# Second attention stage cut into token halves, packed queries loaded two batches at a time

## The chip, the cores and the metric

The kernel runs on one core of one Trainium2 chip. The metric is the device time of one launch in microseconds; of several runs the median is given. Beside it there is one profiled execution, with a time of its own.

## What is computed

A small packed query set p attends to the keys and values, its result serves as keys and values for the full queries q, and two gated layers follow on all tokens.

```python
# q, k, v: (8 batches, 8 heads, 576 tokens, 64); p: (8, 8, 32, 64); float32
def sm_attn(qq, kk, vv):
    s = scale * np.matmul(qq, kk.transpose(0, 1, 3, 2))
    s = s - np.max(s, axis=-1, keepdims=True)
    a = np.exp(s)
    a = a / (np.sum(a, axis=-1, keepdims=True) + 1e-09)
    return np.matmul(a, vv)
p_packed = sm_attn(p, k, v)              # first attention stage
out = sm_attn(q, p_packed, p_packed)     # second attention stage
x = out.transpose(0, 2, 1, 3).reshape(4608, 512)
h = x @ moe_w_in;  x = (h / (1 + np.exp(-h))) @ moe_w_out
h = x @ moe2_w_in; x = (h * np.cos(h)) @ moe2_w_out
# w_in: (512, 2048), w_out: (2048, 512)
```

## The kernel before

Heads are handled in two groups of four (`g` = 0, 1) of each batch `b`. `place_p(b)` loads the packed queries of one batch into `pin` tiles, eight DMAs of 16 KB, and VectorE transposes them into `pbd`. `stage1(b, g)` is the first attention stage: it turns the keys, forms scores against `pbd`, and leaves the packed result in `ppf`. `stage2(b, g)` is the second: it turns q, forms scores of 128 packed rows by 576 tokens in two PSUM banks of 288 tokens, transposes them into 32x32 blocks (`ba` in the first two batches), takes the maximum over 32 (`mxb`), subtracts it, exponentiates on ScalarE, sums (`rsb`), divides, transposes back (`bat`), and splits the result into a rounded tile and its remainder (the two layers of an `a` tile).

The output product of the second stage is folded into the first layer: `products` multiplies `ppf` with w_in, so that `first(s)`, one step of the first layer, is `hb<-a,w` followed by the gate (`gf`, `g`) and `acc<-g,w`. A step takes one block of 288 tokens and one slice of 128 of the 2048 columns. The first pair of batches runs its slices in four parts of four, each over four token blocks: tokens 0 to 287 and 288 to 575 of batch 0, and the same of batch 1. The weights come as words of 64 bits and are decoded on the chip: each slice is loaded (`wd`, `wde`) and takes two ScalarE and three or four VectorE instructions before PE can use it. The second layer (`second`) follows from about half of the span on.

The first two batches run in the class `Boot`: whole rows of k, v and q come into the `bx` tiles by four DMAs of 288 KB each, and PE turns them. From batch 2 on the class `Steady` loads k and q in pieces (`kin`). While PE would otherwise be idle at the start, `fill` puts in products of the identity matrix (`mb<-ident`).

No instruction is issued where the code stands: all are recorded by `Plan`, which gives each a cost (`price`), a due time and its dependences, orders them over all engines by list scheduling, and emits each engine's instructions in that fixed order (`run`). All DMAs stand in the queue of SyncE (SP). Instructions of one engine run strictly in the planned order, so one that waits holds all behind it. A `copy` may go to ScalarE or VectorE; the planner chooses. In the profile nearly all instructions have line 208 (of the recording helper), so tiles are what tells them apart.

Of the kernel before, what the change touches and what calls it, by code (L numbers as in the profile page):

```python
# [12 lines left out]
F32 = mybir.dt.float32  # L13
# [3 lines left out]
AF = mybir.ActivationFunctionType  # L17
ALU = mybir.AluOpType
AX = mybir.AxisListType
# [15 lines left out]
def f32(ap):  # L35

    return ap.bitcast(F32)
# [42 lines left out]
class Plan:  # L80
# [4 lines left out]
    PE, DVE, ACT, POOL, DMA, NONE = "PE", "DVE", "ACT", "POOL", "DMA", "NONE"  # L85
# [72 lines left out]
    def price(self, engine, f, out, ins):  # L158

        n = math.prod(out.shape[1:])  # L160
        m = max([math.prod(x.shape[1:]) for x in ins], default=n)
        sbuf = all(not str(x.space).endswith("PSUM") for x in ins)
        strided = 44 if ins and n >= 96 and ins[0].ap[-1][0] == 2 else 110 if n >= 96 and out.ap[-1][0] > 2 else 0
        if engine == self.PE:
            if f == "transpose":
                return 3 + n / 1.2, 0

            if ins[0].dtype == F32R:
                return n / 2.4 + (18 if n == 512 else 13), 0
            rows, k = out.shape[0], ins[0].shape[0]  # L170
            if rows == 128:
                return n * 3.33 + 10, 0
            if rows == 64:
                return n * 0.82, 0
            return {64: 30 if k == 96 else 37, 288: 65, 512: 117}[n], 0
        if engine == self.DVE:
            if f == "transpose":
                return (67 if sbuf else 160) + n / 0.92, 0
            fast = sbuf and f in ("tensor_copy", "tensor_scalar", "memset") and m == n
            if f == "scalar_tensor_tensor" and sbuf and ins[0].dtype == F32:  # L180
                return 67 + n / 0.53, 0
            return 67 + max(max(m, n) / (1.92 if fast else 0.96), 60 if f == "reciprocal" else 0) + strided, 0
        if engine == self.ACT:
            return (94 if sbuf else 51) + max(m, n) / 1.2 + (190 if f == "accumulate" else 0) + (105 if f == "sin" else 0) + strided, 0
        if engine == self.POOL:
            return 149 + (1.7 if any(0 in [st for st, _ in x.ap] for x in ins) else 2.1) * n, 0
        run = min(map(self.contiguous, (out, *ins)))
        return self.ISSUE, 4 * math.prod(out.shape) / (260 if run >= 128 else 150)
# [217 lines left out]
def attention_mlps_kernel(  # L406
# [13 lines left out]
    B, H, S, D = q.shape  # L420
    NP = p.shape[2]
    NT, DM = out.shape
    DFF = w_in1.shape[1]
    P = 128
    HALF = S // 2

    TA = HALF
    NB = S // 32
# [8 lines left out]
    SCALE = 1.0 / math.sqrt(D)  # L437
# [5 lines left out]
    V, A, T, G, DMA = plan.V, plan.A, plan.T, plan.G, plan.D  # L443
# [4 lines left out]
    def pool(name, side="left", **kw):  # L448
        return tc.tile_pool(name=name, bufs=1, side=side, **kw)

    def ring(ts):

        at = cycle(ts)
        return lambda: next(at)
# [12 lines left out]
    att = top.enter_context(pool("att"))  # L467
# [3 lines left out]
    def tiles(pl, shape, dtype, name, n):  # L471

        ts = [pl.tile(shape, dtype, name=f"{name}{i}") for i in range(n)]
        cells.setdefault(pl, []).extend(t.tensor.name for t in ts)
        return ts


    def place(b, h2):
        return (b + h2) % 2
# [8 lines left out]
    hb = [psum.tile([P, 512], F32, name=f"hb{i}") for i in range(2)]  # L488
# [5 lines left out]
    def group(s):  # L494
        return list(range(4 * s, 4 * s + 4)) + [FC + b * 8 + kc * 4 + s for b in range(2) for kc in range(2)]
# [10 lines left out]
    def change(stack, pools, name, side, new):  # L506


        def f():
            stack.close()  # L510
            pl = ctx.enter_context(pool(name, side, reuse_waits="tile"))
            for x in new:
                x.tile = pl.tile(list(x.ap.shape), x.ap.dtype, name=x.key)

        plan.switch(f, sum([cells[pl] for pl in pools], []), [x.key for x in new])
# [4 lines left out]
    pbds = [const.tile([P, H // 2, 2 * NP], F32, name=f"pbd{i}") for i in range(2)]  # L520
# [7 lines left out]
    def copy(dst, src):  # L528
        with plan.either():
            A.copy(dst, src)  # L530
            V.tensor_copy(dst, src)

    def combine(dst, x, y, op):
        V.tensor_tensor(dst, x, y, op)

    def split(d, x):

        copy(d[:, 0], x)
        combine(d[:, 1], x, f32(d[:, 0]), ALU.subtract)
# [73 lines left out]
        combine(v[1], v[1], v[2], ALU.subtract)  # L613
        put(y[1], 5)

    pins = ring(tiles(att, [P, H // 2, 32], F32, "pin", 2))
    maxes = ring(tiles(att, [P, 2], F32, "mx", 2))
    ms = ring(tiles(att, [P, 1], F32, "m", 2))
    sumss = ring(tiles(att, [P, 1], F32, "sums", 2))
# [1 line left out]
    mx2s = ring(tiles(att, [P, NB], F32, "mxb", 2))  # L621
    rs2s = ring(tiles(att, [P, NB], F32, "rsb", 2))
    ppfs = ring(tiles(att, [P, 2, 2 * NP], F32, "ppf", 4))
    a2s = ring(tiles(a2p, [P, 2, S], F32R, "a2", 4))

    def place_p(b):
        for side in range(2):
            t = pins()
            for h2 in range(2):
                for x in range(2):  # L630
                    r = (h2 ^ side) * 64 + x * 32
                    DMA.dma_start(t[r : r + 32], p[b, h2::2, :, 32 * x : 32 * x + 32].rearrange("j n d -> n j d"))
            for h2 in range(2):
                r, x = slice(64 * (h2 ^ side), 64 * (h2 ^ side) + 64), NP * place(b, h2)
                V.transpose(pbds[b % 2][r, :, x : x + NP], t[r].rearrange("p j d -> p (j d)"))

    def cut(t, shape):
        t = t[:, : math.prod(shape[1:])]
# [5 lines left out]
    class Steady:  # L644

        @staticmethod
        def spot(h2, hf):
            return 64 * (h2 ^ hf), HALF * hf
# [93 lines left out]
    ppf = {}  # L742
    a2 = {}

    def scores(b, keys, queries, bank, spot):

        sts = [bank()[:, :HALF] for _ in range(2)]
        with plan.together():
            for hf, st in enumerate(sts):
                for j in range(2):  # L750
                    for h2 in range(2):
                        (r, c), x = spot(h2, hf), 32 * place(b, h2)
                        T.matmul(
                            st[64 * j + x : 64 * j + x + 32],
                            keys[r : r + 64, j, x : x + 32],
                            queries[j][r : r + 64, c : c + HALF],
                            start=True,
                            stop=True,
                        )
        return sts  # L760
# [50 lines left out]
    def stage2(b, g, bank, mem):  # L811

        qt = mem.turned(q, b, g, bank)
        s = mem.get("s", [P, NB, 32], g)
        sf = s.rearrange("p n r -> p (n r)")
        for hf, st in enumerate(scores(b, ppf[b, g], qt, bank, mem.spot)):
            V.transpose(sf[:, hf * HALF : (hf + 1) * HALF], st)
        mx = mx2s()
        V.tensor_reduce(mx, s, axis=AX.X, op=ALU.max)
        combine(s, s, mx.unsqueeze(2).to_broadcast([P, NB, 32]), ALU.subtract)  # L820
        A.activation(sf, sf, AF.Exp, scale=SCALE)
        rs = rs2s()
        V.tensor_reduce(rs, s, axis=AX.X, op=ALU.add)
        V.tensor_scalar(rs, rs, 1e-9, None, op0=ALU.add)
        V.reciprocal(rs, rs)
        combine(s, s, rs.unsqueeze(2).to_broadcast([P, NB, 32]), ALU.mult)
        at = mem.get("at", [P, S], g)
        V.transpose(at, sf)
        d = a2s()
        split(d, at)  # L830
        a2[b, g] = d


    def mslot(b, kc, s):
# [204 lines left out]
    gt, st, m5s = {}, {}, {}  # L1039
# [80 lines left out]
    boot = Boot()  # L1120
# [8 lines left out]
    def w1_units(s):  # L1129
        ws = [boot_w1() for _ in range(KC)]  # L1130
        for hp in range(KC):
            w1_unit(s, hp, ws[hp])
        return ws
# [10 lines left out]
    V.memset(half_pi, math.pi / 2)  # L1144

    def firsts(b, mem, banks):
        place_p(b)
        for g in range(2):
            stage1(b, g, banks[g], mem)

    def seconds(b):
        for g in range(2):
            stage2(b, g, bank, steady)


    place_p(0)
    boot.load("k", k, 0)
    ws = w1_units(0)
    boot.load("v", v, 0)
    boot.load("q", q, 0)  # L1160
    pairs = [ring([acc[g], acc[2 + g]]) for g in range(2)]
    for g in range(2):
        stage1(0, g, pairs[g], boot)
    for g in range(2):
        stage2(0, g, ring([hb[g], pairs[g]()]), boot)
    products(0, (0,), ws)
    wout1_units(0)
    steady = Steady()
    bank = ring([sb, mb])
    boot.load("k", k, 1)  # L1170
    boot.load("v", v, 1)
    boot.load("q", q, 1)
    firsts(1, boot, [bank, bank])
    products(0, (1,), ws)
    for g in range(2):
        stage2(1, g, bank, boot)
    change(boot_stack, [bpool], "w_b", "right", [W[i] for i in group(1) + group(2)])
    for s in range(1, NG):
        ws = w1_units(s)
# [5 lines left out]
    for b in (2, 3):  # L1185
        firsts(b, steady, [bank, bank])


    for pr in range(NPAIR):
# [14 lines left out]
        for o in range(PAIR[pr + 1] - PAIR[pr]):  # L1204
# [7 lines left out]
            x = o - 48  # L1212
# [51 lines left out]
```

## Time and profile before

| what | value |
|---|---|
| median of 3 runs | 1529.22 us (1528.01 to 1533.76) |
| profiled execution, its own time | 1525.84 us |
| its span, first to last instruction | 1524.1 us |
| PE busy in the span | 1501.3 us, 99% |
| VectorE (DVE) busy | 1150.8 us, 76% |
| ScalarE (ACT) busy | 783.4 us, 51% |
| mean granted TensorE clock | 0.997 of full |

The profiled execution lies 3.4 us below the median of the runs; 1.7 us of it lie outside the span. PE is busy nearly throughout, so what counts is where it isn't, or where it does only fill work: that is the first 100 us.

### The profile page before, as it was taken

Reading aid. Unit: us, or ns where it says so; the run is one execution under the profiler, and the core shown is the slowest. Engines: PE = TensorE matmul, PEld = TensorE weight load, DVE = VectorE, ACT = ScalarE, POOL = GpSimd, SP = SyncE. Lnnn points to the kernel's source line nnn. Section 1 sums busy time; section 2 is a strip of 40 time slices with the busy share of each in tenths; the row PEclk is TensorE's granted clock in tenths of the full one; section 3 lists DMA queues with packets and bytes.
Section 4 is the critical chain, followed back from the end, with each engine's and each line's share of the span. In section 5 each row is a group of like instructions: output and inputs, shape, how many; then the busy total and the mean of one; then the engine's idle time right before and its main releaser. Section 6 shows DMA issues by size and latency. Waiting matters only on the chain.

```text
span 1524.1 us, 30972 instructions
## 1 busy us (share of the span) xinstructions
PE 1501.3 (99%) x11352; PEld 1358.0 (89%) x11352; DVE 1150.8 (76%) x2424; ACT 783.4 (51%) x1683; POOL 0.7 (0%) x6
## 2 busy tenths in 40 slices
PE   8999999999999999999999999999999999999999
PEld 6788878999789998999989999999999999999997
DVE  5998757786788778686377777888887877777665
ACT  5886554555465555555354444544444544444443
POOL 0000000000000000000000000000000000000000
PEclk9899999999999999999999999999999999999999
DMA  8886557555585666453785758778675657575561
GB/s 219 246 250 168 155 113 176 173 131 135 142 229 178 157 138 192 165 189 113 237 256 174 230 178 252 238 232 248 215 216 191 219 174 230 175 230 177 187 191 35
DMA packets 312632, 287.82 MB, mean 189 GB/s; under 512 B 174240, under 2 KB 222880, under 8 KB 312480
## 3 DMA queue, kind: packets, MB, share of 16 engines
q1 hardware_dynamic: 312480, 285.84, 63.0%
q8 instruction: 90, 1.47, 0.4%
q14 instruction: 62, 0.51, 0.1%
HBM read 232.52 MB, written 53.22 MB: 187 GB/s over the span
## 4 chain that ended last, share of the span: by engine, by line
PE 89%; DMA 3%; DVE 2%; SPq 2%; ACT 2%; issue 1%; DVEq 0%; ACTq 0%
PE acc L208 49%; PE hb L208 22%; PE sb L208 10%; PE mb L208 8%; SPq L208 2%; DMA bx<-in_q 1%; DMA wd<-in_moe_w_in 1%; DMA ypart<-ysb 0%; DMA bx<-in_k 0%; DMA bx<-in_v 0%; DMA kin<-in_q 0%; DMA vin<-in_v 0%; DVE r L208 0%; DVE big L208 0%; DVE w L208 0%
## 5 line engine op out<-in xcount | busy, mean ns | idle before, releaser
L208 PE MATMUL acc<-g,w 128*128 128x288 f32 x3072 | 472.1, 297 | 1.6 <-ACT ysb L208 1.1
L208 PEld LDWEIGHTS acc<-g,w 128*128 128x128 f32 x3072 | 425.7, 188 | 30.6 <-issue 19.8
L208 PE MATMUL acc<-w,g 128*128 128x512 f32 x1728 | 431.6, 392 | 0.0
L208 PEld LDWEIGHTS acc<-w,g 128*128 128x128 f32 x1728 | 310.9, 189 | 55.7
L208 PE MATMUL hb<-a,w 128*128 128x288 f32 x1536 | 266.1, 300 | 5.6 <-DVE gf L208 3.7
L208 PEld LDWEIGHTS hb<-a,w 128*128 128x128 f32 x1536 | 223.6, 189 | 21.6 <-issue 8.5
L208 DVE TENSOR_TENSOR g<-gf,g 128x288 fp32r<-128x288 f32 x256 | 115.0, 451 | 59.9 <-PE acc L208 38.7
L208 ACT CAST g<-gf 128x288 fp32r<-128x288 f32 x234 | 101.1, 434 | 112.8 <-PE acc L208 78.3
L208 ACT ACTIVATE gf<-hb 128x288 f32<-128x288 f32 x256 | 103.4, 411 | 101.9 <-PE hb L208 84.1
L208 DVE SCALAR_TENSOR_TENSOR gf<-gf,hb 128x288 f32<-128x288 f32 x256 | 111.6, 449 | 47.8 <-ACT gf L208 46.6
L208 ACT ACTIVATE r<-r,half_pi 128x512 f32<-128x512 f32 x144 | 103.7, 721 | 35.2 <-DVE r L208 35.0
L208 ACT CAST g<-r 128x512 fp32r<-128x512 f32 x144 | 89.5, 621 | 59.0 <-DVE r L208 56.8
L208 PEld LDWEIGHTS hb<-w,w 128*128 128x128 f32 x729 | 103.8, 190 | 7.9
L208 PE MATMUL hb<-w,w 128*128 128x256 f32 x729 | 110.0, 282 | 0.0
L208 DVE TENSOR_TENSOR g<-r,g 128x512 fp32r<-128x512 f32 x144 | 98.8, 687 | 11.0 <-ACT g L208 10.6
L208 DVE SCALAR_TENSOR_TENSOR r<-n,r 128x512 f32<-128x512 int32 x144 | 99.0, 688 | 2.2
L208 ACT ACTIVATE n<-hb 128x512 int32<-128x512 f32 x72 | 43.1, 598 | 112.0 <-PE hb L208 108.3
L208 DVE TENSOR_TENSOR hb<-hb,gf 128x256 f32<-128x256 f32 x72 | 31.1, 432 | 70.9 <-PE hb L208 70.7
L208 ACT ACTIVATE n<-mb 128x512 int32<-128x512 f32 x36 | 21.5, 598 | 93.1 <-PE mb L208 93.1
L208 PE MATMUL mb<-w,w 128*128 128x256 f32 x456 | 65.6, 282 | 0.0
L208 PE MATMUL sb<-w,w 128*128 128x256 f32 x444 | 64.1, 282 | 0.0
L208 DVE TENSOR_SCALAR r<-r 128x512 f32<-128x512 f32 x144 | 60.9, 424 | 2.6
(204 smaller groups left out, 1911.3 us busy)
## 6 DMA issues: line engine op xcount, KB each, us to landing
w<-w2s SPq DMA_DIRECT2D x504, 256.0 KB, 3.6
w2s<-wd SPq DMA_DIRECT2D x28, 512.0 KB, 3.6
wd<-in_moe_w_in SPq DMA_DIRECT2D x24, 512.0 KB, 4.7
w<-w1dram SPq DMA_DIRECT2D x48, 256.0 KB, 3.5
wd<-in_moe_w_out SPq DMA_DIRECT2D x20, 512.0 KB, 4.7
ydram<-ysb SPq DMA_DIRECT2D x64, 144.0 KB, 2.8
raw<-ydram SPq DMA_DIRECT2D x72, 128.0 KB, 3.6
w2dram<-wd SPq DMA_DIRECT2D x16, 512.0 KB, 3.3
```

The lines of the kernel that those rows point to most:

```text
L208: run = lambda: emit(*[real(x) for x in args], **{k: real(x) for k, x in kw.items()})
```

## The change

The second attention stage of a group is written as a function `half(x)` of a token range. For batches 0 and 1 it is called for tokens 0 to 287 and for 288 to 575, later for all 576 at once as before. In batch 0 the first halves of both groups are recorded ahead of the second halves. The packed queries come in `load_p`, once for two batches, into tiles of double size: eight DMAs of 32 KB where two times eight of 16 KB were. Those of batches 0 and 1 are issued by ScalarE, the later ones by SP as before. `load_p(0)` stands behind the load of the keys.

```diff
@@ price
         if engine == self.ACT:
+            if f == "dma_start":
+                return self.ISSUE, 0
...
-    pins = ring(tiles(att, [P, H // 2, 32], F32, "pin", 2))
+    pins = ring(tiles(att, [P, H, 32], F32, "pin", 2))
...
+    def load_p(b):
+        for side in range(2):
+            t = pin[side] = pins()
+            for h2 in range(2):
+                r = 64 * (h2 ^ side)
+                for x in range(2):
+                    (DMA if b else A).dma_start(
+                        t[r + 32 * x : r + 32 * x + 32],
+                        p[b : b + 2, h2::2, :, 32 * x : 32 * x + 32].rearrange("b j n d -> n (b j) d"),
+                    )
...
@@ stage2
-        for hf, st in enumerate(scores(b, ppf[b, g], qt, bank, mem.spot)):
-            V.transpose(sf[:, hf * HALF : (hf + 1) * HALF], st)
-        mx = mx2s()
-        V.tensor_reduce(mx, s, axis=AX.X, op=ALU.max)
-        combine(s, s, mx.unsqueeze(2).to_broadcast([P, NB, 32]), ALU.subtract)
-        A.activation(sf, sf, AF.Exp, scale=SCALE)
...
-        split(d, at)
+        def half(x):
+            k = slice(x.start // 32, x.stop // 32)
+            y = s[:, k]
+            yf = y.rearrange("p n r -> p (n r)")
+            for hf, st in enumerate(sts):
+                a, e = max(x.start, hf * HALF), min(x.stop, hf * HALF + HALF)
+                if a < e:
+                    V.transpose(yf[:, a - x.start : e - x.start], st[:, a - hf * HALF : e - hf * HALF])
+            V.tensor_reduce(mx[:, k], y, axis=AX.X, op=ALU.max)
+            combine(y, y, mx[:, k].unsqueeze(2).to_broadcast([P, k.stop - k.start, 32]), ALU.subtract)
+            A.activation(yf, yf, AF.Exp, scale=SCALE)
+            V.tensor_reduce(rs[:, k], y, axis=AX.X, op=ALU.add)
+            V.tensor_scalar(rs[:, k], rs[:, k], 1e-9, None, op0=ALU.add)
+            V.reciprocal(rs[:, k], rs[:, k])
+            combine(y, y, rs[:, k].unsqueeze(2).to_broadcast([P, k.stop - k.start, 32]), ALU.mult)
+            V.transpose(at[:, x], yf)
+            copy(d[:, 0, x], at[:, x])
+            combine(d[:, 1, x], at[:, x], f32(d[:, 0, x]), ALU.subtract)
+
         a2[b, g] = d
+        return [lambda x=x: half(x) for x in ((slice(0, HALF), slice(HALF, S)) if b < 2 else (slice(0, S),))]
...
-    place_p(0)
     boot.load("k", k, 0)
+    load_p(0)
+    place_p(0)
...
-    for g in range(2):
-        stage2(0, g, ring([hb[g], pairs[g]()]), boot)
+    fs = [stage2(0, g, ring([hb[g], pairs[g]()]), boot) for g in range(2)]
+    for f in sum(map(list, zip(*fs)), []):
+        f()
```

How the planner orders it is seen in each engine's instructions. ScalarE's first ones in the kernel before (`bkt` are turned keys, `pin` the packed queries):

```order
L1259 UNCONDITIONAL_BRANCH
L208 ACT_TABLE_LOAD
L208 COPY bkt_159<-acc_88 128x288
L208 COPY bkt_159<-acc_90 128x288
L208 COPY bkt_160<-acc_88 128x288
```

And in the changed one:

```order
L1286 UNCONDITIONAL_BRANCH
L210 DMA pin_119<-in_p 32x8x32 x4
L210 DMA pin_120<-in_p 32x8x32 x4
L210 ACT_TABLE_LOAD
L210 COPY bkt_159<-acc_88 128x288
```

ScalarE now issues eight DMAs before its first table load and first copy. SP's queue at the start in the kernel before (`bx_156` keys, `bx_157` values, `bx_158` queries; `wd`, `wde` undecoded weights of the first layer):

```order
L208 DMA bx_156<-in_k 96x2x384 x3
L208 DMA pin_119<-in_p 32x4x32 x4
L208 DMA pin_120<-in_p 32x4x32 x4
L208 DMA bx_156<-in_k 96x2x384
L208 DMA bx_157<-in_v 96x2x384 x2
L208 DMA wd_108<-in_moe_w_in 128x1024
L208 DMA wd_109<-in_moe_w_in 128x1024
L208 DMA wde_113<-in_moe_w_in 128x1024
L208 DMA bx_158<-in_q 96x2x384
L208 DMA bx_157<-in_v 96x2x384 x2
L208 DMA wde_114<-in_moe_w_in 128x1024
L208 DMA bx_158<-in_q 96x2x384
```

And in the changed one:

```order
L210 DMA bx_156<-in_k 96x2x384 x4
L210 DMA wd_108<-in_moe_w_in 128x1024
L210 DMA wd_109<-in_moe_w_in 128x1024
L210 DMA bx_157<-in_v 96x2x384 x2
L210 DMA wde_113<-in_moe_w_in 128x1024
L210 DMA bx_157<-in_v 96x2x384 x2
L210 DMA wde_114<-in_moe_w_in 128x1024
L210 DMA bx_158<-in_q 96x2x384 x2
L210 DMA bx_156<-in_k 96x2x384
L210 DMA bx_158<-in_q 96x2x384
```

The eight loads of `pin` are gone from between the third and the fourth load of keys (and eight more, of batch 1, from further down), and all four weights of the first slice group now stand ahead of the first queries. VectorE in the second stage of batch 1, up to the last instruction of group 1 (`a_140`), in the kernel before:

```order
L208 TENSOR_REDUCE rsb_132<-ba_164 128x18
L208 TENSOR_TENSOR ba_163<-ba_163,rsb_131 128x576
L208 TENSOR_SCALAR rsb_132<-rsb_132 128x18
L208 SCALAR_TENSOR_TENSOR wde_114<-wde_114 128x512
L208 RECIPROCAL rsb_132<-rsb_132 128x18
L208 STREAM_TRANSPOSE bat_165<-ba_163 128x576
L208 TENSOR_TENSOR ba_164<-ba_164,rsb_132 128x576
L208 TENSOR_TENSOR g_152<-gf_150,g_152 128x288
L208 STREAM_TRANSPOSE bat_166<-ba_164 128x576
L208 TENSOR_TENSOR a_139<-bat_165,a_139 128x576
L208 TENSOR_SCALAR w_143<-w_143 128x512
L208 TENSOR_TENSOR a_140<-bat_166,a_140 128x576
```

And in the changed one, up to the first half of `a_140`:

```order
L210 TENSOR_SCALAR rsb_132<-rsb_132 128x9
L210 TENSOR_TENSOR a_139<-bat_165,a_139 128x288
L210 RECIPROCAL rsb_132<-rsb_132 128x9
L210 TENSOR_TENSOR ba_164<-ba_164,mxb_130 128x288
L210 TENSOR_TENSOR ba_164<-ba_164,rsb_132 128x288
L210 TENSOR_REDUCE rsb_131<-ba_163 128x9
L210 STREAM_TRANSPOSE bat_166<-ba_164 128x288
L210 TENSOR_TENSOR g_152<-gf_150,g_152 128x288
L210 TENSOR_SCALAR rsb_131<-rsb_131 128x9
L210 TENSOR_REDUCE rsb_132<-ba_164 128x9
L210 SCALAR_TENSOR_TENSOR w_142<-w_142,wd_109 128x512
L210 TENSOR_TENSOR a_140<-bat_166,a_140 128x288
```

In batch 1 the first halves of both groups are done ahead of most of the second halves. In batch 0 they are not: there the two halves of one group follow each other directly, instruction by instruction (`TENSOR_REDUCE mxb_129<-ba_163 128x9 x2`), first those of group 0, then those of group 1. The four transposes of the packed queries of batch 1, which stood among group 0's second stage, now stand at VectorE's very beginning. Over the kernel VectorE has 38 instructions more.

## Rows read from the trace of the kernel before

**Rows 1.** The page, part 1: span, and busy time of each engine.

```profile
span 1524.1 us, 30972 instructions
PE 1501.3 (99%) x11352; PEld 1358.0 (89%) x11352; DVE 1150.8 (76%) x2424; ACT 783.4 (51%) x1683; POOL 0.7 (0%) x6
```

**Rows 2.** Stretches: busy us by engine (instructions), granted clock, DMA share, GB/s.

```profile
core 0: us, PE busy (x) PEld busy (x) DVE busy (x) ACT busy (x) POOL busy (x), PEclk, DMA share, GB/s
...
6.00:8.00 2.00, 2.00 (x19) 1.69 (x18) 0.90 (x3) 1.64 (x5) 0.00 (x0) 1.00 0.15 23
24.00:26.00 2.00, 2.00 (x35) 0.98 (x23) 0.37 (x2) 0.56 (x1) 0.00 (x0) 1.00 0.84 181
26.00:28.00 2.00, 1.54 (x23) 0.84 (x22) 2.00 (x4) 1.52 (x5) 0.00 (x0) 1.00 0.23 44
...
35.00:40.00 5.00, 3.33 (x57) 2.07 (x55) 5.00 (x13) 3.98 (x9) 0.00 (x0) 1.00 1.05 278
...
45.00:50.00 5.00, 4.49 (x27) 3.34 (x15) 4.93 (x16) 4.80 (x12) 0.00 (x0) 0.50 1.08 240
50.00:60.00 10.00, 10.00 (x111) 7.99 (x110) 7.52 (x16) 7.49 (x17) 0.00 (x0) 0.84 1.04 309
...
80.00:100.00 20.00, 18.40 (x146) 17.40 (x147) 19.98 (x43) 17.71 (x42) 0.00 (x0) 1.00 0.80 242
100.00:600.00 500.00, 492.66 (x4441) 445.75 (x4439) 384.98 (x846) 278.26 (x652) 0.00 (x0) 1.00 0.61 161
```

**Rows 3.** SP's DMA issues in order of time: start, duration, tile, count.

```profile
2.16 4.75 SPq L208 DMA_DIRECT2D pin<-in_p  x8
...
6.96 0.43 SPq L208 DMA_DIRECT2D bx<-in_k  x1
...
19.82 7.58 SPq L208 DMA_DIRECT2D pin<-in_p  x7
27.70 0.31 SPq L208 DMA_DIRECT2D bx<-in_q  x1
```

**Rows 4.** The chain that ended last, near its beginning and around 48 us.

```profile
12.67 13.58 DMA bx<-in_q
...
48.08 1.81 PE hb L208 x6
```

**Rows 5.** ScalarE in order of time: the fourth weight load's decoding, idle before.

```profile
25.44 0.67 ACT L208 ACTIVATE wde<-wde 128x512 int32<-128x512 uint32 x1 [2.91 <-DMA wde<-in_moe_w_in]
```

**Rows 6.** VectorE's groups by shape, 0 to 150 us: busy, mean ns, idle before.

```profile
L208 DVE STREAM_TRANSPOSE pbd<-pin 64x128 f32<-64x128 f32 x12 | 3.5, 298 | 6.8 <-DMA pin<-in_p 6.7
...
L208 DVE STREAM_TRANSPOSE bat<-ba 128x576 f32<-128x576 f32 x4 | 3.0, 755 | 0.0
L208 DVE TENSOR_TENSOR ba<-ba,mxb 128x576 f32<-128x576 f32 x4 | 3.0, 752 | 0.0
...
L208 DVE TENSOR_REDUCE mxb<-ba 128x18 f32<-128x576 f32 x4 | 2.9, 733 | 0.0
...
L208 DVE RECIPROCAL rsb<-rsb 128x18 f32<-128x18 f32 x4 | 1.0, 258 | 0.0
...
L208 DVE STREAM_TRANSPOSE ba<-mb 128x288 f32<-128x288 f32 x2 | 0.9, 442 | 0.0
```

**Rows 7.** ScalarE's groups by shape, 0 to 150 us.

```profile
L208 ACT ACTIVATE gf<-hb 128x288 f32<-128x288 f32 x36 | 14.8, 415 | 4.0 <-PE hb L208 1.8 <-DVE g L208 1.8
...
L208 ACT ACTIVATE ba<-ba 128x576 f32<-128x576 f32 x4 | 2.8, 698 | 0.0
```

**Rows 8.** VectorE and PE in order of time, second stage of batch 1.

```profile
63.45 0.48 DVE L208 STREAM_TRANSPOSE ba<-sb 128x288 f32<-128x288 f32 x1 [0.25 <-ACT w L208]
...
75.52 0.71 DVE L208 TENSOR_TENSOR ba<-ba,rsb 128x576 f32<-128x576 f32 x1
...
76.16 0.45 DVE L208 TENSOR_TENSOR g<-gf,g 128x288 fp32r<-128x288 f32 x1
...
76.36 0.53 PE L208 MATMUL hb<-a,w 128*128 128x288 f32 x2 [0.36 <-ACT a L208]
76.52 0.77 DVE L208 STREAM_TRANSPOSE bat<-ba 128x576 f32<-128x576 f32 x1
...
78.28 0.76 DVE L208 TENSOR_TENSOR a<-bat,a 128x576 fp32r<-128x576 f32 x1
...
81.60 1.85 PE L208 MATMUL hb<-a,w 128*128 128x288 f32 x12 [1.71 <-DVE gf L208]
```

More of the change, by code (lines that the diff above doesn't have):

```diff
@@ L624, in attention_mlps_kernel @@
     a2s = ring(tiles(a2p, [P, 2, S], F32R, "a2", 4))
+    pin = {}
+    def load_p(b):
[8 more added lines that the diff above has]
+                    )
     def place_p(b):
         for side in range(2):
[L628 to L632, printed above, removed]
             for h2 in range(2):
                 r, x = slice(64 * (h2 ^ side), 64 * (h2 ^ side) + 64), NP * place(b, h2)
-                V.transpose(pbds[b % 2][r, :, x : x + NP], t[r].rearrange("p j d -> p (j d)"))
+                t = pin[side][r, b % 2 * (H // 2) : (b % 2 + 1) * (H // 2)]
+                V.transpose(pbds[b % 2][r, :, x : x + NP], t.rearrange("p j d -> p (j d)"))
     def cut(t, shape):
@@ L814, in stage2 @@
         s = mem.get("s", [P, NB, 32], g)
-        sf = s.rearrange("p n r -> p (n r)")
-        for hf, st in enumerate(scores(b, ppf[b, g], qt, bank, mem.spot)):
-            V.transpose(sf[:, hf * HALF : (hf + 1) * HALF], st)
-        mx = mx2s()
-        V.tensor_reduce(mx, s, axis=AX.X, op=ALU.max)
-        combine(s, s, mx.unsqueeze(2).to_broadcast([P, NB, 32]), ALU.subtract)
-        A.activation(sf, sf, AF.Exp, scale=SCALE)
[L822 to L826, printed above, removed]
-        at = mem.get("at", [P, S], g)
-        V.transpose(at, sf)
-        d = a2s()
-        split(d, at)
+        at = mem.get("at", [P, S], g)
+        mx, rs, d = mx2s(), rs2s(), a2s()
+        sts = scores(b, ppf[b, g], qt, bank, mem.spot)
+        def half(x):
[16 more added lines that the diff above has]
+            combine(d[:, 1, x], at[:, x], f32(d[:, 0, x]), ALU.subtract)
         a2[b, g] = d
+        return [lambda x=x: half(x) for x in ((slice(0, HALF), slice(HALF, S)) if b < 2 else (slice(0, S),))]
     def mslot(b, kc, s):
@@ L1146, in firsts @@
     def firsts(b, mem, banks):
+        if b % 2 == 0:
+            load_p(b)
         place_p(b)
@@ L1152, in seconds @@
         for g in range(2):
-            stage2(b, g, bank, steady)
+            for f in stage2(b, g, bank, steady):
+                f()
+    boot.load("k", k, 0)
+    load_p(0)
     place_p(0)
-    boot.load("k", k, 0)
     ws = w1_units(0)
@@ L1163, in attention_mlps_kernel @@
         stage1(0, g, pairs[g], boot)
-    for g in range(2):
-        stage2(0, g, ring([hb[g], pairs[g]()]), boot)
+    fs = [stage2(0, g, ring([hb[g], pairs[g]()]), boot) for g in range(2)]
+    for f in sum(map(list, zip(*fs)), []):
+        f()
     products(0, (0,), ws)
@@ L1175, in attention_mlps_kernel @@
     for g in range(2):
-        stage2(1, g, bank, boot)
+        for f in stage2(1, g, bank, boot):
+            f()
     change(boot_stack, [bpool], "w_b", "right", [W[i] for i in group(1) + group(2)])
```

## The prediction, written before the changed kernel was run

> **What bounds the kernel now.** I read the page's first part, then the stretches, then the chain, and went to the timeline only where these pointed. The page says that PE is busy 1501.3 of 1524.1 us [rows 1]: a change that leaves PE's work alone can win back 22.8 us of gaps at most, plus what PE loses to a lowered clock. The stretches say where the gaps are: from 100 to 600 us PE is busy 492.66 of 500 us [rows 2], so most of what can be won or lost lies ahead of 100 us, and that is also where the halves act. In that part PE is not the one that sets the pace. Up to 26 us the chain runs over the load of the queries: a DMA issued at 12.67 us ends 13.58 us later, at 26.25 us [rows 4]. Afterwards VectorE has nearly no idle time (2.00 of 2 us at 26 to 28, 4.93 of 5 us at 45 to 50, 19.98 of 20 us at 80 to 100) while PE is idle 1.6 us of the last of these [rows 2]. From 48.08 us on the chain enters PE's own work [rows 4], while PE's granted clock is 0.50, half rate [rows 2]; before it fell, PE had been idle a third of the time (3.33 of 5 us busy at 35 to 40 [rows 2]). So three things can be moved: the loads up to 26 us, VectorE's packed stretch up to 48 us, and the waits of PE for batch 1 near 76 to 82 us.
>
> **The loads.** SP needed 4.75 us to issue eight loads of packed queries, and the fourth load of keys came behind them at 6.96 us; the DMA share fell to 0.15 between 6 and 8 us. The loads for batch 1 held SP from 19.82 us for 7.58 us (seven of them), the third load of queries came behind them at 27.70 us, and the share was 0.23 between 26 and 28 us [rows 2, 3]. Both holes close when the sixteen issues leave SP's queue. The first is worth 2.0 x 0.85 = 1.7 us of DMA time ahead of the queries that the chain waits for. Against it, 128 KB more packed queries are on the way early, half a microsecond at the 250 GB/s of a full stretch. What stands ahead of the second query load in SP's order is otherwise the same loads in another order. I take 1.0 us (bounds 0 and 1.7) for the first scores of batch 0. The second hole lets group 1's queries, batch 1's keys and the next weights come some 2 us earlier, but VectorE is packed by then, so I count nothing for it (bounds 0 and 1.5).
>
> Issuing costs ScalarE what it cost SP, some 4.75 us before its first copy. That delays the turned keys by up to that time; the cover is the wait for queries until 26.25 us. Without that cover it would cost up to 4.75 us. ScalarE's exponential of group 0 now also stands behind the first weight's decoding, so it waits for that load; the same cover holds. No compute instruction waits in SP's queue for these loads any more.
>
> The fourth weight load now precedes the first queries, so it lands about a query load (288 KB, 1.2 us) and the closed hole earlier than 25.44 us, where ScalarE had sat 2.91 us for it [rows 5]. Its decoding then falls where VectorE has little to do (0.37 of 2 us busy at 24 to 26 [rows 2]), and the 512-wide subtraction that stood inside group 0's second stage goes ahead of it: some 0.7 us out of the packed stretch (estimated by the 0.71 us of a 576-wide one).
>
> **The halves.** Each group had eight VectorE instructions behind the score transposes: six of 576 elements, of 0.733 to 0.755 us, and two small ones of at most 0.258 us [rows 6]. In halves the six become twelve of about 0.45 us (442 ns for a transpose, 0.45 us for a product of 288 [rows 6, 8]) and the small ones four. By durations that is 6 x (0.90 - 0.745) = 0.93 and about 0.35 us for the small ones: 1.3 us a group, 5.1 us over four groups. But durations overlap: from start to start a 576-wide one took 76.16 - 75.52 = 0.64 us and a 288-wide one 76.52 - 76.16 = 0.36 us [rows 8], which gives 6 x 0.08 + 0.35 = 0.8 us a group, 3.4 us in all. In a packed queue start to start is what counts, but one pair is little; I take 1.0 us a group, 4.0 us in all, and keep 3.4 and 5.1. ScalarE's exponential goes from 0.698 to 2 x 0.415 us [rows 7], with the rounding copy about 0.3 us a group more; ScalarE has room in the packed stretches (17.71 of 20 us at 80 to 100 [rows 2]), so I count nothing (bound 1.3 us).
>
> [...]
>
> *Batch 0.* The packed stretch from the first scores to 48 us starts 1.0 us earlier; four transposes of packed queries (4 x 0.298 = 1.2 us [rows 6]) move to the beginning, where VectorE waited for the loads anyway (6.7 us in two waits), and 0.7 us of weight work goes ahead. Two groups in halves add 2.0 us. Since the halves follow each other directly in VectorE's order, PE gets its first full block hardly ahead of the second. Net: -1.0 - 1.2 - 0.7 + 2.0 = **-0.9 us** (bounds -3.9 and +1.4).
>
> *Batch 1.* From its first score transpose at 63.45 us to the end of the last `a` instruction at 79.04 us VectorE took 15.6 us [rows 8]. In the new order 36 instructions reach from the same transpose to group 1's first half: 27 of 288 elements at 0.36 to 0.40 us, four of the weights' decoding at about 0.5 us, five small ones at 0.2 us: about 13.3 us, 2.3 us less. PE waited there 0.36 us for group 0 and 1.71 us behind the new batch's first steps [rows 8], so at most 2.07 us can come back. The second halves then come about 3 us later than before, beneath four steps of PE on the first halves; but VectorE remains full until 100 us, and two groups' 2.0 us of added work stay in its queue ahead of the gates that PE needs. I take half of it, 1.0 us, as returned in waits. Net: -2.07 + 1.0 = **-1.1 us** (bounds -2.1 and +3.0).
>
> *Afterwards.* The later batches have the same instructions, with half as many load issues for the packed queries. PE's 7.3 us of gaps in 100 to 600 us [rows 2] are shuffled a little by the planner: 0, within 2 us either way.
>
> Sum: -0.9 - 1.1 = **-2.0 us**, 1523.8 us for the profiled execution's 1525.84 us. That execution lies 3.4 us below the median of the runs, so against the median of 1529.22 us the forecast is **1527 us**.
>
> **Rivals.** (1) *Everything early carries through.* The packed stretch of batch 0 gets all of its 3.9 us, batch 1 all of its 2.1 us, and PE's half-rate stretch, which cost it 2.6 us from 48 us on where the chain was PE's (0.50 until 50 us and, at a mean of 0.84, 3.2 us more [rows 2]; half of 5.2 us), falls away because PE has its first blocks sooner: 8.6 us, 1520.6 us. For it: the two DMA holes are real, and PE's gaps are what preceded the low clock. Against it: VectorE is as full as before, and in batch 0 the halves are not apart.
> (2) *The cut costs what it adds.* VectorE is the bound from 26 to 100 us, the 5.1 us stay in its queue, and what PE gains on first halves it gives back waiting for gates. Place: 60 to 100 us. Price: +5.1 us, with nothing from the loads, 1534.3 us; it is decided by whether VectorE, full in 80 to 100 us, catches up before 100 us, or stays full beyond some 110 us. [...] For a loss of more than 0.5% a second half-rate stretch would have to fall on PE's own work as well.
> (3) *The loads do nothing.* ScalarE's late start (up to 4.75 us) delays the keys, the queries' wait hides both this and the closed hole, and only batch 1 counts: 1528 us.
>
> **How the numbers follow.** 0.5% is 7.6 us, about what a measurement of this kernel can tell from no change. Chances: the forecast, with its neighbourhood from -5 to +2 us, 0.58; the loads alone 0.12; everything early 0.16; the cost of the cut 0.14. Of everything early some 0.11 passes -7.6 us, of the cost of the cut 0.06 passes +7.6 us. That gives 0.11, 0.83 and 0.06. The range reaches from 1520 us, rival (1), to 1534 us, rival (2).
>
> **What would show it.** Right: no DMA hole at 6 to 8 and at 26 to 28 us; queries of batch 0 landed near 25 us; PE's first `hb<-a` steps with both groups near 45 us; PE's waits at 76 to 82 us down to under 1 us; some 30 to 40 more VectorE instructions ahead of 100 us, with VectorE full until there. Wrong: ScalarE's first copy so late that the scores of batch 0 come after 28 us; the half-rate stretch gone, or a second one in PE's dense part; VectorE still full beyond 110 us with PE waiting for gates; or a difference from 100 us on that has nothing to do with the halves.

## The result, and the profile after

The changed kernel took 1538.91 us (median of 6 runs, 1534.66 to 1540.08) beside 1529.5 us for the kernel before: ratio 1.0055 [1.0035, 1.0075]. It is slower by 0.55%, about 8 us, and outside the predicted range of 1520 to 1534 us. The profiled execution took 1537.19 us (before: 1525.84 us). The page's first part, as in [rows 1]:

```profile
span 1535.4 us, 30938 instructions
PE 1514.0 (99%) x11352; PEld 1370.8 (89%) x11352; DVE 1155.3 (75%) x2462; ACT 780.6 (51%) x1685; POOL 0.7 (0%) x6
```

PE has exactly as many instructions as before (11352), but they took 12.7 us more, while the span grew by 11.3 us. Summed over the span PE does not wait longer: it works more slowly. The stretches say where (columns as in [rows 2]):

```profile
6.00:8.00 2.00, 0.87 (x10) 0.68 (x8) 0.94 (x5) 0.48 (x1) 0.00 (x0) 1.00 1.18 243
8.00:10.00 2.00, 0.74 (x5) 0.74 (x6) 0.50 (x3) 1.99 (x5) 0.00 (x0) 0.75 0.95 331
10.00:12.00 2.00, 2.00 (x12) 1.33 (x10) 0.00 (x0) 1.64 (x5) 0.00 (x0) 0.50 1.01 327
24.00:26.00 2.00, 2.00 (x13) 2.00 (x13) 0.28 (x1) 0.94 (x2) 0.00 (x0) 0.50 1.13 272
26.00:28.00 2.00, 2.00 (x12) 2.00 (x12) 0.41 (x1) 0.70 (x2) 0.00 (x0) 0.50 0.72 206
...
40.00:45.00 5.00, 4.98 (x47) 2.47 (x39) 1.40 (x3) 2.45 (x6) 0.00 (x0) 0.69 1.07 292
...
50.00:60.00 10.00, 8.28 (x76) 6.17 (x79) 9.25 (x30) 7.71 (x20) 0.00 (x0) 0.50 0.51 156
60.00:80.00 20.00, 19.40 (x190) 15.52 (x185) 17.30 (x42) 17.45 (x42) 0.00 (x0) 0.82 0.28 93
80.00:100.00 20.00, 19.81 (x169) 17.95 (x168) 19.46 (x57) 17.90 (x46) 0.00 (x0) 1.00 0.65 186
100.00:600.00 500.00, 493.32 (x4459) 448.30 (x4458) 390.59 (x858) 279.65 (x659) 0.00 (x0) 1.00 0.61 164
```

Between 6 and 10 us PE is busy 1.61 of 4 us; in the second half of that the granted clock falls from 1.00 to 0.50, and it comes back only within 40 to 45 us. At 24 to 28 us, where before VectorE was beginning to be packed, PE is full, VectorE nearly empty (0.41 of 2 us), and PE takes fills and the transposes of the first stage (`acc<-ident,ba`) in turn, where the kernel before had got to the second stage's scores (27.3 us). A second half-rate stretch fills 50 to 60 us and reaches on into the next row (0.82 for 60 to 80 us, where the kernel before had 1.00): cut finer, it lasts until 67 us. Before, there was one such stretch, from 43 to 53 us. Later nothing is lost: at 80 to 100 us PE's gaps shrank from 1.60 to 0.19 us, and 100 to 600 us is as full as before. The timeline says what PE lacked (start, duration, instruction, idle before it and what ended it; ACTq and SPq are the DMA issues of ScalarE and SyncE):

```profile
0.74 6.75 ACTq L210 DMA_DIRECT2D pin<-in_p  x8
0.74 4.25 SPq L210 DMA_DIRECT2D bx<-in_k  x4
...
7.52 1.28 ACT L210 ACT_TABLE_LOAD   x1 [7.52 <-DMA pin<-in_p]
...
8.81 3.07 ACT L210 COPY bkt<-acc 128x288 f32<-128x288 f32 x8
...
9.26 2.18 PE L210 MATMUL acc<-ident,bx 96*128 96x96 f32 x12 [2.39 <-ACT bkt L210]
...
13.19 0.50 DVE L210 STREAM_TRANSPOSE pbd<-pin 64x128 f32<-64x128 f32 x2 [4.69 <-DMA pin<-in_p]
...
13.55 1.21 PE L210 MATMUL acc<-bkt,pbd 64*32 64x288 f32 x14 [1.00 <-DVE pbd L210]
```

ScalarE's eight issues took 6.75 us, not the 4.75 us that they took on SP [rows 3]; the table load stands behind them, and the first copy of turned keys begins at 8.81 us. PE waits 2.39 us for it, because the four `acc` banks are full. The last packed queries are ready to be transposed only at 13.19 us: PE waits another 1.00 us. The chain has the two loads, too, and behind them PE's own work, fill (`mb`) first, in place of the query load of [rows 4]:

```profile
1.70 5.45 DMA pin<-in_p
7.17 5.92 DMA pin<-in_p
16.52 4.46 PE mb L210 x20
30.95 3.61 PE mb L210 x16
```

What it delays is seen at PE's second-stage scores of batch 0 (`hb<-bkt,ppf`; durations min/median/max in ns, first and last start). Before:

```profile
L208 PE MATMUL hb<-bkt,ppf x16: 402/415/427, 27.3 to 35.4; 64*32 64x288 f32 x16
```

And after, where the first of them comes 14.8 us later, ahead of any half of a token range:

```profile
L210 PE MATMUL hb<-bkt,ppf x16: 402/403/682, 42.1 to 48.4; 64*32 64x288 f32 x16
```

Theories from this profile. **A**: the issue on ScalarE opens gaps on PE, the clock falls to half, and PE's fixed order, with 40 fills ahead of the scores, takes twice as long. **B**: the halves' added VectorE work costs the time. **C**: loading two batches at once does, whoever issues. Later a fourth one came up: the lateness of keys and queries alone, without the clock.

### The profile page after: what moved, and what is told of

Its sections match the earlier page's. It is cut to its first block, busy times and chain, and to the rows that moved or that the text cites. A ratio compares the mean times of both kernels' runs of the same rounds, so it can differ in the third digit from the quotient of the medians.

```text
span 1535.4 us, 30938 instructions
## 1 busy us (share of the span) xinstructions
PE 1514.0 (99%) x11352; PEld 1370.8 (89%) x11352; DVE 1155.3 (75%) x2462; ACT 780.6 (51%) x1685; POOL 0.7 (0%) x6
## 4 chain that ended last, share of the span: by engine, by line
PE 87%; DVE 5%; DMA 4%; ACT 1%; SPq 1%; issue 1%; ACTq 0%; DVEq 0%
PE acc L210 48%; PE hb L210 21%; PE sb L210 9%; PE mb L210 9%; DMA ysb<-ypart 2%; SPq L210 1%; DVE r L210 1%; DMA pin<-in_p 1%; DMA kin<-in_q 1%; DVE g L210 1%; DMA ypart<-ysb 0%; DVE w L210 0%; DVE raw L210 0%; DMA kin<-in_k 0%; DMA wd<-in_moe_w_out 0%
```

## The experiments

All ratios are to the kernel before on the same chip, with 95% intervals. Except where it is said, a changed kernel is planned anew, so that its instructions can also stand in another order.

**1. Which part.** All packed queries issued by SP, the rest of the change kept:

```diff
-                    (DMA if b else A).dma_start(
+                    DMA.dma_start(
```

> The changed kernel, with its two-batch loads of packed queries all issued by SP (one word of the code); the halves stay. Theory A (ScalarE's issue: its 6.75 us of issuing delay the first copies to 8.8 us and the last packed queries to 13.2 us, PE gets gaps, and runs at half rate from 9 us on): ScalarE's first copy back near 5.5 us, the last transpose of packed queries near 9 to 10 us, no half rate ahead of 30 us, 1523 to 1531 us. Theory B (the halves' added VectorE work is the loss): as the changed kernel, 1536 to 1541 us. Theory C (loading two batches at once is the loss, whoever issues it): 1534 to 1540 us.

The halves alone (`load_p` and its wide tiles undone):

> The kernel before with the token halves alone; the packed queries as before, a batch at a time from SP. Theory A: 1522 to 1530 us, the halves worth -6 to 0 us. Theory B: 1536 to 1541 us. Theory C: like A.

The loads alone (`half` undone in `stage2`):

> The kernel before with the new loads alone (two batches at a time, the first from ScalarE), the second stage whole. Theory A: half rate from about 9 us on as in the changed kernel, 1538 to 1545 us, since the halves' gain is missing. Theory B: 1526 to 1531 us. Theory C: 1536 to 1545 us.

Measured: loads from SP 1524.23 us, 0.9963 [0.995, 0.9976]; halves alone 1521.13 us, 0.9947 [0.9928, 0.9966]; loads alone 1552.3 us, 1.0149 [1.0127, 1.017]. B falls: without the halves the kernel is slower still, and the halves alone gain 8 us. C falls: with SP issuing the same loads the loss is gone. The same change issued by SP is 0.92% faster than issued by ScalarE (0.9963 for 1.0055). The timeline with the loads alone shows the gap, longer than in the changed kernel:

```profile
0.73 7.17 ACTq L210 DMA_DIRECT2D pin<-in_p  x8
...
9.22 0.70 ACT L210 COPY bkt<-acc 128x288 f32<-128x288 f32 x2
...
9.68 1.22 PE L210 MATMUL acc<-ident,bx 96*128 96x96 f32 x6 [3.43 <-ACT bkt L210]
```

And with SP issuing, where no such gap is left and all eight transposes of packed queries run from 8.20 us on:

```profile
2.66 5.18 SPq L210 DMA_DIRECT2D pin<-in_p  x8
...
5.95 1.92 ACT L210 COPY bkt<-acc 128x288 f32<-128x288 f32 x6 [3.94 <-PE acc L210]
...
7.65 0.69 PE L210 MATMUL acc<-ident,bx 96*128 96x96 f32 x6 [0.26 <-ACT bkt L210]
...
8.20 1.93 DVE L210 STREAM_TRANSPOSE pbd<-pin 64x128 f32<-64x128 f32 x8 [7.34 <-DMA pin<-in_p]
```

There the second-stage scores of batch 0 start at 27.0 us:

```profile
L210 PE MATMUL hb<-bkt,ppf x16: 402/402/428, 27.0 to 31.5; 64*32 64x288 f32 x16
```

**2. A planner that knows the price.** The planner reckoned 0.5 us for such an issue and nothing until the data landed. Here it is told more, and orders anew:

```diff
             if f == "dma_start":
-                return self.ISSUE, 0
+                return 840, 5000
...
+        if a.engine == self.ACT and a.issue:
+            return other + a.issue
```

> The changed kernel, with the planner told what a load from ScalarE costs here: 0.84 us of ScalarE and 5 us until it has landed, in place of 0.5 us and none. Data and loads stay; the planner puts fifteen fill products ahead of the first scores. Theory A in its form that the half rate does the harm: PE busy up to 13 us, no half rate before 30 us, 1525 to 1533 us. Theory A in its form that the lateness itself does it: still 1535 to 1540 us, at full rate. Theory B: 1536 to 1541 us whatever the clock.

Measured: 1527.4 us, 0.9986 [0.9972, 1.0]. The planner gave the first five copies of keys to VectorE and put 15 fills ahead of the first scores; the second-stage scores start at 33.4 us. The clock fell here too, against the expectation (0.95 at 12 to 16, 0.50 from 16 to 24 us), so this run does not separate clock and order. The eight issues on ScalarE are still there (6.87 us), so most of the loss is not the issues themselves but an order that doesn't reckon with them.

**3. Half the dose.** Four of the eight loads on ScalarE, four on SP behind the keys:

```diff
-                    (DMA if b else A).dma_start(
+                    (DMA if b or side else A).dma_start(
```

> The changed kernel with only the first four of the eight loads of queries issued by ScalarE, the other four by SP behind the keys: half the dose. Theory A with gaps as the trigger: ScalarE is free some 2.5 to 3.4 us earlier, its first copy comes at about 5.6 to 6.5 us, no gap of 2.4 us opens on PE, the clock stays at full rate beyond 20 us and the time is near that of the kernel with all eight on SP, 1522 to 1528 us. Rival (each load on ScalarE's queue costs its share, whatever the gaps): half of the loss stays, 1530 to 1533 us.

Measured: 1521.13 us, 0.9953 [0.9936, 0.997], at full rate up to 36 us and with second-stage scores from 28.2 us. The loss is no share of the dose. Four issues took 1.94 us, not half of 6.75 us, and the first copy came at 6.08 us:

```profile
0.73 1.94 ACTq L210 DMA_DIRECT2D pin<-in_p  x4
...
0.73 1.87 SPq L210 DMA_DIRECT2D bx<-in_k  x4
...
4.62 2.20 SPq L210 DMA_DIRECT2D pin<-in_p  x4
...
6.08 2.40 ACT L210 COPY bkt<-acc 128x288 f32<-128x288 f32 x6 [2.09 <-PE acc L210]
```

**4. The clock alone.** The sharpest test of A keeps the eight issues and the order and fills only the gaps, with identity products put into PE's instructions at emission, unseen by the planner. It took three attempts. `more(op, at, n)` inserts n fills at place `at` of a recorded block:

```diff
+    def more(op, at, n):
+        op.emit[at:at] = [lambda: nc.tensor.matmul(mb[:, :64], ident, ident[:, :64], start=True, stop=True)] * n
...
                             T.transpose(st[:, m * CH : (m + 1) * CH], pair, ident[:CH, :CH])
+                    if src is k and b == 0 and j:
+                        more(plan.ops[-1], 0, 2 if g or h2 else 20)
...
+        if b == 0 and keys.tensor.name == pbds[0].tensor.name:
+            more(plan.ops[-1], 4, 10)
+            more(plan.ops[-1], 2, 10)
```

> The changed kernel with PE's order kept word for word, and 66 small fills (128x64) put into the gaps that ScalarE's eight issues leave: 20 ahead of the second half of the key transposes, 2 ahead of each of the next three groups, 20 inside each of the first two blocks of scores. Nothing of the change is undone. If the half rate that these gaps bring on is the price (theory A), the stretch at half rate from 9.0 us is gone or much shorter, the second stage's first scores come at 30 to 35 us in place of 42.1, and the time falls by 6 to 12 us, to 1527 to 1533 us. If it is the lateness alone (rival: first copy at 8.8, last queries at 13.2, and everything behind them keeps its distance), the scores stay at 40 us or later and the time within 3 us of the changed kernel's 1538.9 us.

Measured: 1537.5 us, 1.0057 [1.0038, 1.0077]: what the rival expected, although the clock stayed at 1.00 until past 45 us. The fills were mis-sized. Each shows as two instructions, and the timeline has the first twenty of them take 4.58 us:

```profile
6.78 4.58 PE L761 MATMUL mb<-ident 128*128 128x64 f32 x40
11.19 0.42 PE L210 MATMUL acc<-ident,bx 96*128 96x96 f32 x3
```

66 of them are some 15 us of work, about what the half rate had cost; the scores came at 41.5 us. The run does not separate clock from lateness; it shows only that 15 us of added work in PE's order delay the scores as much. The next one has 20 fills (10, three times 1, and 7 in the first scores):

```diff
-                        more(plan.ops[-1], 0, 2 if g or h2 else 20)
+                        more(plan.ops[-1], 0, 1 if g or h2 else 10)
...
-            more(plan.ops[-1], 4, 10)
-            more(plan.ops[-1], 2, 10)
+            more(plan.ops[-1], 2, 0 if ppf or plan.scored else 7)
+            plan.scored = True
```

> The run with 66 extra fills put 15 us of PE work of its own into the order (a fill lasts 0.23 us at full rate, twice what was reckoned), which took the place of the half rate. Here 20 extra fills, 4.6 us, stand where PE waits anyway: 10 in the gap before 9.26 us, 1 ahead of each of three groups, 7 in the wait for the last packed queries. PE's order is otherwise the changed kernel's. If half rate on the fixed order (with its 40 fills) is the loss: no half rate before 30 us, the work from the scores of batch 0's first stage to those of its second, 27 us at half rate, takes some 15 us, these scores come at 29 to 32 us in place of 42.1, and the time is 1523 to 1530 us. If the lateness of ScalarE's issue alone is it: scores at 38 us or later, 1535 us or more.

Measured: 1540.69 us, 1.0084 [1.0069, 1.0098]. Again not the test that was meant: the 7 fills stood behind the matmul that waits, as the timeline shows, and the scores came at 46.5 us.

```profile
14.36 0.67 PE L210 MATMUL acc<-bkt,pbd 64*32 64x288 f32 x2 [2.60 <-DVE pbd L210]
14.96 3.15 PE L762 MATMUL mb<-ident 128*128 128x64 f32 x14
```

PE stood idle for 2.60 us, and the fills behind took 3.15 us for 7, half rate (the clock is 1.00 at 14 to 15 us, 0.55 at 15 to 16 and 0.50 at 16 to 20). So the fall was only put off, and the fills came on top. In the third attempt 11 fills stand one matmul earlier, inside the wait:

```diff
-            more(plan.ops[-1], 2, 0 if ppf or plan.scored else 7)
+            more(plan.ops[-1], 1, 0 if plan.scored else 11)
```

> The run with 20 extra fills had 7 of them behind the matmul that waits for the last packed queries, so that PE still stood idle for 2.60 us before 14.36 us and the clock fell there. Here the 11 fills of that place (2.6 us at full rate) stand one matmul earlier, inside the wait; the other 13 as before; PE's order is otherwise the changed kernel's, with its 40 fills and all eight loads on ScalarE. If the half rate is what makes the changed kernel late: no half rate before 30 us, 27 us of PE work shrink to some 15, second-stage scores at 29 to 32 us, 1524 to 1531 us. If lateness comes with full rate too: scores after 37 us, over 1534 us.

Measured: 1526.79 us, 1.0002 [0.9988, 1.0015]. The stretches, at full rate where the changed kernel has 0.50 (up to 35 us no row is below 1.00; between 35 and 50 us the means are 0.90, 0.76 and 0.66):

```profile
10.00:12.00 2.00, 2.00 (x18) 1.42 (x16) 0.00 (x0) 1.53 (x5) 0.00 (x0) 1.00 1.07 340
...
24.00:26.00 2.00, 2.00 (x51) 1.93 (x53) 0.29 (x2) 0.27 (x1) 0.00 (x0) 1.00 1.12 276
...
50.00:60.00 10.00, 9.89 (x118) 7.79 (x119) 9.38 (x22) 9.25 (x22) 0.00 (x0) 1.00 0.78 251
```

The timeline, with the added fills inside the wait:

```profile
11.08 0.67 PE L210 MATMUL acc<-bkt,pbd 64*32 64x288 f32 x2
11.68 2.67 PE L762 MATMUL mb<-ident 128*128 128x64 f32 x22
14.27 0.71 PE L210 MATMUL acc<-bkt,pbd 64*32 64x288 f32 x14
```

And the second-stage scores:

```profile
L210 PE MATMUL hb<-bkt,ppf x16: 400/402/428, 30.0 to 35.4; 64*32 64x288 f32 x16
```

ScalarE still issues eight loads (6.81 us), its first copy still comes at 8.87 us and the last queries at 13.50 us, and 24 products were added. Yet the scores start 12.1 us sooner (30.0 for 42.1), and by the ratios the kernel is 0.53% faster than the changed one: the whole loss against the kernel before. What differs is the clock.

It is not all that the issue on ScalarE costs. Issued by SP, the same change stands at 0.9963 [0.995, 0.9976], and its scores start 3.0 us sooner still. Of the 0.92% between the two ways of issuing, keeping the clock up brought back 0.53%. The other 0.4% can be the lateness itself, the 24 products, or the order, which is another one with SP; no run separates these. By the two profiled spans (1521.5 and 1520.2 us) it is only 1.3 us, but the profiled execution of the third attempt, 1523.3 us, lies 3.5 us below its median.

**5. What the half rate acts on.** The changed kernel without its 40 planned fills (all else as planned anew):

```diff
-    fill(8000, 20000, 300, 64)
```

> The changed kernel without the 40 fills that are recorded for 8 to 20 us; eight loads by ScalarE as in the change. The half rate stays (the gaps are only longer), but PE's order no longer holds the 18 us of fills at half rate. If it is the fills in the fixed order that turn half rate into lateness: second-stage scores at 28 to 33 us though the clock is at half, and a time of 1524 to 1531 us. If half rate slows the chain itself, or the issue's lateness holds it: scores after 36 us and 1533 us or more.

Measured: 1528.13 us, 1.0005 [0.9994, 1.0016]. The clock is at 0.50 here as well (0.50 from 12 to 20 us, 0.52 at 20 to 24), and PE waits even longer, 3.05 us for the last queries; yet PE comes through:

```profile
9.36 1.70 PE L210 MATMUL acc<-ident,bx 96*128 96x96 f32 x12 [1.90 <-ACT bkt L210]
10.99 1.17 PE L210 MATMUL acc<-bkt,pbd 64*32 64x288 f32 x2
15.21 2.17 PE L210 MATMUL acc<-bkt,pbd 64*32 64x288 f32 x30 [3.05 <-DVE pbd L210]
```

Its second-stage scores start at 32.8 us. So half rate costs as much as it does because the order holds fill work ahead of the scores. How much is in the groups by shape from 7.5 to 45 us (busy us, mean ns); in the changed kernel

```profile
L210 PE MATMUL mb<-ident 128*128 128x64 f32 x80 | 19.5, 405 | 0.0
```

and in the same order at full rate, the third attempt of the fourth experiment,

```profile
L210 PE MATMUL mb<-ident 128*128 128x64 f32 x80 | 10.6, 268 | 0.0
```

That is 8.9 us of the 12.1 us from the same 40 fills. By the other groups of this view the kernel's own products lose some 6 us at half rate; against that the third attempt has 5.4 us of added products, and 0.5 us of waits where the changed kernel has 3.4 us.

**6. Are the fills of use at all?** The kernel with four loads on ScalarE, without the 40 fills (the same line taken out):

> The kernel with four loads on ScalarE and four on SP, without the 40 fills recorded for 8 to 20 us: does full rate there need them, and is their place in PE's order a price even at full rate (9 us of PE work)? If they only fill waits: the clock falls to half between 10 and 25 us and the time is 1522 to 1527 us, later than with them (1521). If they hold the chain also at full rate: 1517 to 1520 us.

Measured: 1525.58 us, 0.9995 [0.9983, 1.0008], later than with them (0.9953), as expected of fills that keep the rate: the clock falls to a mean of 0.63 at 16 to 20 and 0.51 at 20 to 24 us, where it is 1.00 with them. But the second-stage scores came at 26.8 us, 1.4 us sooner than with fills (28.2). So the scores alone do not set the time. Of the 0.42%, 3.0 us are there at the last `ypart` store, which ends the first pair's partial sums (246.6 for 243.6 us); what loses them after the scores stays open.

**7. Where the halves gain.** In batch 1 alone and in batch 0 alone, old loads (`b < 2` becomes `b == 1` or `b == 0`):

> The kernel before with the token halves in batch 1 alone, old loads. By the prediction's terms batch 1 was worth 1.1 us (bounds -2.1 to +3.0) and batch 0 0.9 us (-3.9 to +1.4), while both together measured 8 us by medians and 3.5 us by profiles. If batch 1 carries the gain: 1521 to 1524 us. If batch 0 does: 1527 to 1530 us. If it needs both: between.

> The kernel before with the token halves in batch 0 alone, old loads. The mirror of the run with batch 1 alone: 1521 to 1524 us if batch 0 carries the gain of the halves, 1527 to 1530 us if batch 1 does; in the first case the first store of the activations moves ahead of its 66.3 us and the waits of PE from 26 to 60 us get shorter.

Measured: batch 1 alone 1528.81 us, 0.9998 [0.9983, 1.0013]; batch 0 alone 1523.52 us, 0.9959 [0.9941, 0.9977]. By the times batch 0 carries most of the 8 us (0.41 of 0.53%), and batch 1 no gain that can be told from zero. The profiles agree only in part. The last `ypart` store starts at 250.8 us before, 248.4 with batch 1, 248.8 with batch 0 and 245.7 us with both: up to there each gives 2.0 to 2.4 us, and they add. At the second layer's first `n<-mb` the four stand at 766.0, 765.8, 763.4 and 762.2 us: batch 1's gain is lost again in between. The first store of activations did not move ahead (67.2 us for batch 0 alone, 66.3 before), against the expectation; from 26 to 60 us PE is busy 29.11 us for 28.52 us, at a mean clock of 0.80 for 0.85, so its gaps there shrank by 0.6 us.

## Why the prediction was wrong

**The step that failed** is in the part on the loads: "Issuing costs ScalarE what it cost SP, some 4.75 us before its first copy ... the cover is the wait for queries until 26.25 us." The issue took 6.75 us, and the table load stood behind it, but the first copy came at 8.81 us for 5.57 before: 3.2 us later, within the 4.75 us that the text allows for. What failed was the cover. The wait for queries could hide ScalarE's late start only if no other engine lost by it; here PE stood still for 2.39 and 1.00 us, the clock fell, and PE's order from the first scores to the second stage, 40 fills included, became longer than the wait for queries that was to cover it. The fourth experiment shows that the clock makes up the loss against the kernel before (0.53%), though not all that the issue on ScalarE costs (0.92%); the fifth, that the fills are the greater part of what it acts on. The text named both signs that appeared ("the scores of batch 0 come after 28 us", a second half-rate stretch in the dense part) and said that a larger loss would need such a stretch, but it put that, at 0.06, under the cost of the cut; the loads had no rival in which they cost time, and a failed cover was priced at 4.75 us at most.

**The DMA holes** closed as told (share 1.18 for 0.15 at 6 to 8 us, 0.72 for 0.23 at 26 to 28 us), but in the changed kernel another opened at once, 0.08 at 28 to 30 us, where SP waited 9.7 us for the late PE (`acc`). Closing them was worth little: with SP issuing the wide loads, the scores start at 27.0 us for 27.3, where 1.0 us was taken, and the time is no better than with the halves alone (0.9963 and 0.9947). The issuing time, 4.75 us on SP [rows 3], was not saved but moved, and grew to 6.75 us in front of an engine that others wait for.

**The halves** were priced with the wrong sign in batch 0. In the text's terms they add 2.0 us there and win 1.1 us in batch 1, together a cost of 0.9 us; the forecast gain of 2.0 us rested on the loads and what moves with them (1.0 + 1.2 + 0.7 us). The runs show the reverse: halves alone 0.9947, some 8 us faster by the medians, 3.5 us by the two spans (1520.6 and 1524.1), and loads alone 1.0149. Durations were as taken (288-wide instructions of 433 to 467 ns for "about 0.45 us") and the 38 added instructions came. Rival (2), the cut costs what it adds, is refuted by the halves alone. The waits of PE behind `gf` fell from 2.2 to 0.9 us (26 to 110 us, halves alone), as the part on batch 1 had it, and batch 1 alone (0.9998 [0.9983, 1.0013]) does not contradict its -1.1 us. But batch 0, taken as a cost, holds most of the gain. Why, and why a gain at 250 us does not last until 766 us, stays open.

**Rival (1)** asked for the half-rate stretch to fall away; instead one came at 8 to 10 us, long ahead of the old one. **Rival (3)**, the loads do nothing, had ScalarE's late start in it and hid it under the same wait. Two bounds of the working do not come out of its terms: batch 0's own give -3.4 (-1.7, -1.5, -1.2, -0.7 and half of 3.4), not the -3.9 that rival (1) uses, and batch 1's +3.0 is not added up. Neither would have reached the measured time.

**What else stays open.** Loads alone cost 22 us and halves alone gain 8 us, but together they cost 8 us, not 14. In the profiles the loads alone are 7 us behind the changed kernel at the first `ypart` store (131.1 and 124.1 us) and 16.5 us at the second layer's start (792.1 and 775.6 us); what is lost in between was not tried. The clock may not be the whole of it: one of the four executions of the loads alone has a mean granted clock of 0.993, the others 0.979 to 0.982, and it took as long (1551.88 us). There is no trace of it.

**A kernel that beats both:** the halves with four loads on ScalarE and four on SP (1521.13 us, 0.9953) or with the old loads (1521.13 us, 0.9947); the two cannot be told apart.

## What to carry to other kernels

When a step is moved to another engine, look at what that engine does first and who waits for it, then ask whether PE stands idle in that wait: gaps of 2.4 and 1.0 us delayed PE by 12 us here, because what PE's fixed order held afterwards, fill work too, ran at half rate until 43 us. Fill work helped here where it stood inside the wait, ahead of the instruction that waits (1526.79 us); one instruction later it only added to the order (1540.69 us). A planner that reckons 0.5 us for an issue, and nothing until the data have landed, planned such a gap itself here.

## What the runs showed of the hardware that was not expected

The time that a row of issues holds its engine was not proportional to their number. Four on ScalarE beside four on SP took 1.94 and 1.87 us; eight on ScalarE beside four on SP took 6.75 and 4.25 us. A single issue lasted about the same (median 475 ns of the four, 449 ns of the eight), so between them the engine stood still for some 3 us, for which the trace shows no wait:

```profile
L210 ACTq DMA_DIRECT2D pin<-in_p x8: 318/449/481, 0.7 to 7.2; - x8
...
DMA to landing us min/median/max: 3.6/5.1/5.9
```

On SP alone, eight of the same size behind four loads of keys took 5.18 us, and all were transposed without a further wait from 8.20 us on; from ScalarE the last ones were there at 13.19 us, though their issue ended no later (7.49 and 7.84 us). In all of these the twelfth issue, of keys and packed queries together, ended at about the same time, whichever engine issued how many: 6.82 us for four and four (SP began its loads of packed queries only at 4.62 us), 7.39 before [rows 3], 7.49 in the changed kernel, 7.84 from SP alone. For the landing a rival stands untested: in the changed kernel SP issued two loads of weights, of 512 KB each, from 6.00 us on, while the last packed queries were still to land; with SP issuing everything, these weights waited until 7.88 us. What holds the issue, and the landing, was not settled.
